# Gated mix of Hedgehog linear attention and a squared-ReLU layer: key features times values taken for two chunks of rows at a time

## The chip, the cores and the metric

The kernel runs on one core of one Trainium2 chip. The metric is device time in microseconds (us). A core has five engines that run side by side and wait for each other by semaphores: PE (TensorE, matmuls; its weight loads have a row of their own, PEld), DVE (VectorE), ACT (ScalarE), POOL (GpSimd) and SP, which here only issues DMAs. Matmuls write to PSUM, eight banks of 128 partitions x 512 floats; the other data lie in SBUF, 128 partitions wide.

## What is computed

The input x has 2048 rows of 512. Two branches are mixed with a gate per row:

```python
qkv = (x @ wqkv) -> q, k, v              # 32 heads of 16
pq, pk = q @ w_phi, k @ w_phi            # per head, 16 x 16
phi(p) = concat(softmax(p), softmax(-p)) # 32 features per head
kv = phi(pk)^T v ; z = sum over rows of phi(pk)
o = (phi(pq) kv) / (phi(pq) z + 1e-6)
a = o @ wo
b = relu(x @ w1 + b1)^2 @ w2 + b2        # 512 -> 1792 -> 512
g = sigmoid(sum(x * gate_w))
out = g * a + (1 - g) * b
```

All is in 32-bit floats. The attention has no mask, so kv and z are sums over all 2048 rows and must be complete before the first query is used.

## The kernel before

**Precision.** Large products are made in three matmuls of a faster 32-bit form: each operand is split into a high part and the low rest, and `mm3` (lines 66 to 70) adds high x high (line 68), high x low (69) and low x high (70). Lines 68 to 70 therefore stand for most of PE's time, and tiles tell apart what they belong to: `u` is the up projection x @ w1, `d` the down projection, `k`, `v`, `q` the projections of keys, values and queries, `att` the output projection. The split itself is line 60 (high part, ACT) and line 63 (low part, DVE). The feature map's weight is folded into the key and query weights beforehand (`fold`, line 142).

**Tiling and stages.** The rows are cut into 4 blocks of 512, each of 4 chunks of 128. The hidden layer's 1792 columns are cut into 14 tiles of 128, half of them per sweep. The program makes two sweeps over the rows. In each, a list of 28 steps (4 blocks x 7 hidden tiles) runs, and a step does the up projection of a hidden tile two steps ahead and the down projection of its own. Between these, the attention's work is laid by hand: `at(slot, f, ...)` puts a piece of it at a half step (lines 464 to 508), so that PE finds it in its stream between up and down projections. A scheduler then places the instructions of each engine by their dependencies and priorities; `high_priority` and `issue_after` guide it. The first sweep carries the keys and values of all 16 chunks (block b, chunk c, n = 4 b + c), the second one the queries, numerators and the output projection.

**Around the change, per chunk n of the first sweep:**

- `do_k` (lines 400 to 402): the key projection into a PSUM bank, then `exps` (191 to 210): DVE takes per head the maximum and the minimum and subtracts (lines 199 to 202) into the tile `e`, 128 x 1024; ACT takes the exponential in place (204), DVE sums it and inverts the sums (207, 209), and POOL scales `e` in place (213). The result is the chunk's key features, `phi`. The tile `e` has two buffers.
- `do_v` (404 to 407): the value projection into the same bank (there is one for this work in the first sweep, as the second bank holds the sums); ACT copies it to `vext`, in which each head has 16 values and a column of ones, set once at the start by POOL (line 126). There are two `vext` tiles, used in turn.
- `do_kv` (409 to 412) calls `kv_chunk` (217 to 224): 32 small matmuls, one per head, each with 17 columns of weights (`vext` of the head) and 32 moving columns (`phi` of the head), in four column groups of the array. All chunks add into one PSUM tile, `kvps`. They are written in plain 32-bit floats, and in the profile each of the 32 is two records of line 221. Such a run of 64 records is called a burst here.

The slots of the three are 5 + 2.9 n for `do_k`, 2 later for `do_v` and 5 later for `do_kv`, in half steps.

After the last burst `kv_done` (423 to 443) copies the sums out on DVE (line 428), sends the row of z through DRAM by SP's queue and back to all partitions (431, 434), transposes the sums on PE (439) and copies them to `kvb` (443). Then `q_phi` (226 to 243) makes the query features: the same `exps`, then POOL multiplies them by z (line 231, tile `ez`, one buffer), and so on to the row's denominator. `transposed` (247 to 257) turns them by a DVE transpose and copies, of which SP issues twelve per chunk as DMAs (line 257). `numer` (263 to 287) takes the numerators by 32 narrow matmuls of two records each per pair of chunks (line 268).

Of the kernel before, what the change touches and what calls it, by code (L numbers as in the profile page):

```python
# [8 lines left out]
F32 = mybir.dt.float32  # L9
F32R = mybir.dt.float32r  # L10
AF = mybir.ActivationFunctionType
# [5 lines left out]
P = 128  # L17
S, D, H, DH, F = 2048, 512, 32, 16, 1792
# [3 lines left out]
NC = SB // P  # L22
# [2 lines left out]
LAG = 2  # L25
NG = 8
VW = DH + 1
AHEAD = 150


@with_exitstack
def tile_gated_mix(ctx: ExitStack, tc: tile.TileContext, xT, xn, wqT, wkT, wphi, wv, wo, w1, b1, w2, b2, gw, out):
    nc = tc.nc
    pool = lambda name, bufs, **kw: ctx.enter_context(tc.tile_pool(name=name, bufs=bufs, **kw))
# [5 lines left out]
    work = pool("work", 2)  # L40
    small = pool("small", 3)
# [8 lines left out]
    def bank(name):  # L50
        p = banks[taken[0] % len(banks)]
        taken[0] += 1
        return p.tile([P, 512], F32, tag="s", name=name)
# [4 lines left out]
    def split(src, hi, lo, ehi, elo):  # L58
        if ehi is nc.scalar:
            i = nc.scalar.activation(hi, src, AF.Copy)  # L60
        else:
            i = ehi.tensor_copy(hi, src)
        elo.tensor_tensor(lo, src, hi.bitcast(F32), ALU.subtract)  # L63
        return i

    def mm3(o, a, b, sa, sb, first, last):
        (ah, al), (bh, bl) = a, b
        nc.tensor.matmul(o, ah[:, sa], bh[:, sb], start=first, stop=False)  # L68
        nc.tensor.matmul(o, ah[:, sa], bl[:, sb], start=False, stop=False)  # L69
        return nc.tensor.matmul(o, al[:, sa], bh[:, sb], start=False, stop=last)  # L70
# [36 lines left out]
        return xs  # L107

    st, up_w, down_w = {}, {}, {}
    hold = pool("hold", 2)  # L110
    ident = const.tile([P, P], F32, name="ident")
    make_identity(nc, ident)
    b1c = const.tile([P, NF], F32, name="b1c")
# [6 lines left out]
    nc.gpsimd.memset(kvb, 0.0)  # L120
    part = dram.tile([NB * NC, P, D], F32, name="part")
    zrow = dram.tile([2 * D], F32, name="zrow")
    vext = [hold.tile([P, H * VW], F32, tag="vz", name=f"vext{i}") for i in range(2)]
    heads = lambda v: v.rearrange("p (h v) -> p h v", v=VW)
    for v in vext:
        nc.gpsimd.memset(heads(v)[:, :, DH:VW], 1.0)
    zbc = []
# [10 lines left out]
    def fold(loaded, nm, k):  # L138
# [6 lines left out]
        lo = wpool.tile([P, 512], F32R, tag=f"wal{k}", name=f"w{nm}l{k}")  # L145
        with tc.high_priority(offset=AHEAD):
            split(ps, hi, lo, nc.scalar, nc.vector)
# [36 lines left out]
    def project(c, xs, ws, nm):  # L184
        ps = bank(nm)
        sc = slice(c * P, (c + 1) * P)
        for k in range(NK):
            mm3(ps, xs[k], ws[k], sc, ALL, k == 0, k == NK - 1)
        return ps

    def exps(ps):

        pv = ps.rearrange("p (h f) -> p h f", f=DH)
        mx = small.tile([P, H], F32, tag="mx", name="mx")
        mn = small.tile([P, H], F32, tag="mn", name="mn")
        e = work.tile([P, H, 2, DH], F32, tag="e", name="e", bufs=2)
        bc = lambda t: t.unsqueeze(2).to_broadcast([P, H, DH])
        with tc.high_priority(offset=AHEAD):
            nc.vector.tensor_reduce(mx, pv, AX.X, ALU.max)  # L199
            nc.vector.tensor_reduce(mn, pv, AX.X, ALU.min)  # L200
            nc.vector.tensor_tensor(e[:, :, 0, :], pv, bc(mx), ALU.subtract)
            nc.vector.tensor_tensor(e[:, :, 1, :], bc(mn), pv, ALU.subtract)  # L202
        ef = e.rearrange("p h t f -> p (h t f)")
        nc.scalar.activation(ef, ef, AF.Exp)  # L204
        e3 = e.rearrange("p h t f -> p (h t) f")
        sm = small.tile([P, 2 * H], F32, tag="sm", name="sm")
        nc.vector.tensor_reduce(sm, e3, AX.X, ALU.add)  # L207
        r = small.tile([P, 2 * H], F32, tag="r", name="r")
        nc.vector.reciprocal(r, sm)  # L209
        return e3, r  # L210

    def scaled(e3, w, eng):
        eng.tensor_tensor(e3, e3, w.unsqueeze(2).to_broadcast([P, 2 * H, DH]), ALU.mult)  # L213
        return e3.rearrange("p h f -> p (h f)")


    def kv_chunk(n, kvps, phi, v):
        for i in range(NG):
            for j in range(4):
                h = 8 * (i % 4) + 4 * (i // 4) + j  # L220
                nc.tensor.matmul(kvps[32 * j:32 * j + VW, 32 * i:32 * i + 32], v[:, h * VW:(h + 1) * VW],  # L221
                                 phi[:, 32 * h:32 * h + 32],
                                 start=(n == 0 and i == 0), stop=(n == NB * NC - 1),
                                 skip_group_check=True)

    def q_phi(n, ps):
        e3, r = exps(ps)
        ez = work.tile([P, 2 * H, DH], F32, tag="ez", name="ez", bufs=1)
        for half in range(2):
            hs = slice(half * H, (half + 1) * H)  # L230
            nc.gpsimd.tensor_tensor(ez[:, hs, :], e3[:, hs, :], zbc[half], ALU.mult)  # L231
        dz = small.tile([P, 2 * H], F32, tag="dz", name="dz")
        nc.vector.tensor_reduce(dz, ez, AX.X, ALU.add)
        nc.vector.tensor_tensor(dz, dz, r, ALU.mult)
        d2 = dz.rearrange("p (h t) -> p h t", t=2)
        den = small.tile([P, H], F32, tag="den", name="den")
        nc.vector.scalar_tensor_tensor(den, d2[:, :, 0], 1e-6, d2[:, :, 1], ALU.add, ALU.add)
        nc.vector.reciprocal(den, den)
        nc.vector.tensor_scalar(den, den, gate[:, n:n + 1], None, ALU.mult)
        w = small.tile([P, H, 2], F32, tag="w", name="w")  # L240
        nc.vector.tensor_tensor(w, r.rearrange("p (h t) -> p h t", t=2),
                                den.unsqueeze(2).to_broadcast([P, H, 2]), ALU.mult)
        return scaled(e3, w.rearrange("p h t -> p (h t)"), nc.vector)
# [19 lines left out]
    def numer(pt):  # L263
# [17 lines left out]
        for r in range(2):  # L281
            oh = work.tile([P, 512], F32R, tag=f"oh{r}", name="oh", bufs=1)
            ol = work.tile([P, 512], F32R, tag=f"ol{r}", name="ol", bufs=1)
            with tc.high_priority(offset=AHEAD):
                split(pss[r], oh, ol, nc.scalar, nc.vector)
# [112 lines left out]
            st["x", b] = load_x(b % NB)  # L398

    def do_k(b, c):  # L400
        e3, r = exps(project(c, st["x", b], st["wa"], "k"))
        st["phi", c] = scaled(e3, r, nc.gpsimd)

    def do_v(b, n, c):
        ps = project(c, st["x", b], st["wb"], "v")
        with tc.high_priority(offset=AHEAD):
            nc.scalar.activation(heads(vext[n % 2])[:, :, :DH], ps.rearrange("p (h f) -> p h f", f=DH), AF.Copy)

    def do_kv(n, c):
        if n == 0:  # L410
            st["kv"] = ps_b.tile([P, 2 * P], F32, tag="s", name="kvps")
        kv_chunk(n, st["kv"], st["phi", c], vext[n % 2])

    def do_q(b, n, c):
        phi = q_phi(n, project(c, st["x", b], st["wa"], "q"))
        if c % 2 == 0:
            st["pt", n // 2] = work.tile([P, 2, 4, NG, 32], F32, tag="phiT", name="phiT", bufs=1)
        transposed(phi, st["pt", n // 2], c % 2)
# [4 lines left out]
    def kv_done():  # L423
        kvps, kvs = st["kv"], row()[:, :2 * P]
        nc.gpsimd.memset(kvs, 0.0)
        for j in range(4):
            s = slice(32 * j, 32 * j + VW)
            nc.vector.tensor_copy(kvs[s, :], kvps[s, :])
# [3 lines left out]
        for half in range(2):  # L432
            z = hold.tile([P, H * VW], F32, tag="vz", name=f"z{half}")[:, :D]
            nc.sync.dma_start(z, zrow[half * D:(half + 1) * D].partition_broadcast(P))
# [10 lines left out]
    def finish(n, c):  # L445
# [5 lines left out]
        t = st["f", n]  # L451
        with tc.high_priority(offset=AHEAD):
            nc.vector.tensor_tensor(t, ps, t, ALU.add)
# [10 lines left out]
    def at(slot, f, *a):  # L464
        steps.setdefault(int(slot), []).append(lambda: f(*a))
# [10 lines left out]
    for b in range(NB):  # L476
        for c in range(NC):
            s = b * SL + 3 * c - 3 if b else 7 + c
            at(s, gate_load, b * NC + c)
            at(s + 3, gate_chunk, b * NC + c)  # L480
        at(b * SL + 4, do_x, b + 1)
        for c in range(NC):
            n = b * NC + c
            s = 5 + 2.9 * n
            at(s, do_k, b, c)
            at(s + 2, do_v, b, n, c)
            at(s + 5, do_kv, n, c)
    base = (NB - 1) * SL
    at(46, do_wT, wqT)
    for k in range(NK):  # L490
# [8 lines left out]
    for p in range(NB * NC // 2):  # L499
        n, s = 2 * p, 54 + 6 * p  # L500
# [30 lines left out]
    for t, (sw, b, i) in enumerate(work_list):  # L531
# [14 lines left out]
        for c in range(NC):  # L546
            n = b * NC + c
# [10 lines left out]
            for j, s in enumerate(halves if n == NB * NC - 1 and done else (ALL,)):  # L558
                with tc.high_priority(offset=AHEAD):
                    nc.vector.scalar_tensor_tensor(o[:, s], dps[c][:, s], rest[:, n:n + 1], o[:, s], ALU.mult, ALU.add)  # L560
# [49 lines left out]
```

## Time and profile before

| | us |
|---|---|
| median of 3 runs | 533.31 |
| lowest and highest of them | 532.88, 533.75 |
| the profiled execution, its own time | 533.63 |
| its span in the profile | 531.8 |

| engine | busy us | share of the span |
|---|---|---|
| DVE | 355.9 | 67% |
| ACT | 234.7 | 44% |
| POOL | 76.8 | 14% |

A row of a timeline gives the start from the span's beginning, the length, the engine, the line, the operation, output and inputs with their sizes, how many instructions it merges, and in brackets the engine's idle time before it with what released it. The length of a merged row goes from the first start to the last end, and instructions of PE overlap: their starts tell the pace, their lengths hold what is in the pipe. A row of a group gives after its shape the count, then busy us and mean ns of one, then the engine's idle time before such instructions. The sixteen bursts start at 59.86, 68.91, 83.39, 97.88, 112.37, 126.85, 141.34, 155.83, 170.31, 184.80, 202.10, 211.15, 225.63, 240.12, 256.34 and 270.88 us.

### The profile page before, as it was taken

How to read it: one execution, taken by the hardware profiler on the slowest of the kernel's cores; microseconds unless marked ns; L12 is line 12 of the kernel's file. 1: busy time of each engine (PE TensorE's matmuls, PEld its weight loads, DVE VectorE, ACT ScalarE, POOL GpSimd, SP SyncE). 2: the span in 40 equal slices, each digit the busy share in tenths (PEclk: the TensorE clock that was granted, in tenths of full speed). 3: DMA queues.
4: the chain of work that ended last, by engine and by line, in shares of the span. 5: the costliest groups of instructions: out<-in, count | busy, mean ns of one | idle time of the engine just before them, and what ended most of it. 6: DMA issues, size and time to landing. Idle time of an engine off the chain costs nothing.

```text
span 531.8 us, 8944 instructions
## 1 busy us (share of the span) xinstructions
PE 521.5 (98%) x3475; PEld 417.5 (79%) x3475; DVE 355.9 (67%) x608; ACT 234.7 (44%) x404; POOL 76.8 (14%) x60
## 2 busy tenths in 40 slices
PE   8998999999999999999999999999999999999997
PEld 3886888888888887887878878787887878787775
DVE  4688536743465434567579998998878887779423
ACT  3874333622435224254654564353435353535230
POOL 2001111111110011011103121202111111112000
PEclk9999999999999999999999999999999999999999
DMA  7974004200042000415346113134102311023102
GB/s 236 297 240 138 2 0 160 76 6 1 1 159 70 10 1 21 160 41 160 88 139 222 35 41 122 53 118 137 40 22 79 119 51 30 22 70 100 49 1 79
DMA packets 30834, 45.16 MB, mean 85 GB/s; under 512 B 5704, under 2 KB 12360, under 8 KB 30792
## 3 DMA queue, kind: packets, MB, share of 16 engines
q1 hardware_dynamic: 30328, 44.20, 27.0%
q8 instruction: 27, 0.44, 0.3%
q10 hardware_dynamic: 432, 0.39, 0.2%
q14 instruction: 15, 0.12, 0.1%
q0 software_dynamic: 32, 0.01, 0.0%
HBM read 29.89 MB, written 8.39 MB: 72 GB/s over the span
## 4 chain that ended last, share of the span: by engine, by line
PE 72%; DVE 10%; DMA 6%; SPq 5%; ACT 3%; POOL 2%; issue 2%; DVEq 0%; ACTq 0%; POOLq 0%
PE u L68 7%; PE d L69 7%; PE d L70 7%; PE d L68 7%; PE u L70 7%; PE u L69 7%; SPq L257 4%; PE v L68 3%; PE k L68 3%; PE v L69 3%; PE v L70 3%; PE k L70 3%; PE k L69 3%; PE kvps L221 2%; DMA in<-in_xT 2%; PE att L68 2%
## 5 line engine op out<-in xcount | busy, mean ns | idle before, releaser
L303 ACT ACTIVATE r<-u,b1c 128x512 f32<-128x512 f32 x56 | 38.5, 687 | 151.3 <-PE u L70 148.0
L68 PE MATMUL d<-w2h,hh 128*128 128x512 f32 x224 | 87.5, 391 | 0.0
L69 PE MATMUL d<-w2l,hh 128*128 128x512 f32 x224 | 87.3, 390 | 0.0
L70 PE MATMUL d<-w2h,hl 128*128 128x512 f32 x224 | 87.1, 389 | 0.0
L68 PE MATMUL u<-xh,w1h 128*128 128x512 f32 x220 | 86.8, 395 | 0.1
L70 PE MATMUL u<-xh,w1l 128*128 128x512 f32 x220 | 85.7, 390 | 0.5 <-DVE w1l L63 0.5
L69 PE MATMUL u<-xl,w1h 128*128 128x512 f32 x220 | 85.8, 390 | 0.0
L63 DVE TENSOR_TENSOR hl<-r,hh 128x512 fp32r<-128x512 f32 x56 | 43.0, 769 | 54.8 <-ACT hh L60 54.7
L231 POOL TENSOR_TENSOR ez<-e,z 128x512 f32<-128x512 f32 x32 | 41.4, 1317 | 188.3 <-ACT e L204 188.3
L213 POOL TENSOR_TENSOR e<-e,r 128x1024 f32<-128x1024 f32 x16 | 32.3, 2017 | 205.0 <-DVE r L209 158.3
L207 DVE TENSOR_REDUCE sm<-e 128x64 f32<-128x1024 f32 x32 | 39.0, 1218 | 28.5 <-ACT e L204 28.4
L68 PEld LDWEIGHTS u<-xh,w1h 128*128 128x128 f32 x220 | 41.3, 188 | 12.0 <-issue 1.6
L70 PEld LDWEIGHTS d<-w2h,hl 128*128 128x128 f32 x224 | 42.0, 188 | 8.7
L68 PEld LDWEIGHTS d<-w2h,hh 128*128 128x128 f32 x224 | 42.0, 188 | 8.7
L69 PEld LDWEIGHTS d<-w2l,hh 128*128 128x128 f32 x224 | 42.1, 188 | 8.6
L70 PEld LDWEIGHTS u<-xh,w1l 128*128 128x128 f32 x220 | 41.3, 188 | 9.5 <-DVE w1l L63 0.9
L69 PEld LDWEIGHTS u<-xl,w1h 128*128 128x128 f32 x220 | 41.3, 188 | 8.2
L204 ACT ACTIVATE e<-e 128x1024 f32<-128x1024 f32 x32 | 33.8, 1055 | 23.7 <-DVE e L202 23.5
L255 ACT ACTIVATE phiT<-tb 32x256 f32<-32x256 f32 x64 | 26.5, 413 | 35.1 <-DVE tb L249 34.4
L60 ACT ACTIVATE hh<-r 128x512 fp32r<-128x512 f32 x56 | 35.2, 628 | 1.3
L304 ACT ACTIVATE r<-r 128x512 f32<-128x512 f32 x56 | 35.1, 627 | 1.0
L199 DVE TENSOR_REDUCE mx<-k 128x32 f32<-128x512 f32 x16 | 11.0, 688 | 26.3 <-PE k L70 26.3
(106 smaller groups left out, 888.5 us busy)
## 6 DMA issues: line engine op xcount, KB each, us to landing
in<-in_xT SPq DMA_DIRECT2D x32, 256.0 KB, 3.9
in<-in_w SPq DMA_DIRECT2D x24, 256.0 KB, 3.2
phiT<-tb SPq DMA_DIRECT2D x192, 32.0 KB, 1.8
row<-in_xn SPq DMA_DIRECT2D x16, 256.0 KB, 3.2
part<-row SPq DMA_DIRECT2D x16, 256.0 KB, 2.0
row<-part SPq DMA_DIRECT2D x16, 256.0 KB, 3.5
out<-row SPq DMA_DIRECT2D x15, 256.0 KB, 2.2
row<-in_wkT SPq DMA_DIRECT2D x4, 256.0 KB, 6.0
```

What stands on the lines that cost most here:

```text
L60: i = nc.scalar.activation(hi, src, AF.Copy)
L63: elo.tensor_tensor(lo, src, hi.bitcast(F32), ALU.subtract)
L68: nc.tensor.matmul(o, ah[:, sa], bh[:, sb], start=first, stop=False)
L69: nc.tensor.matmul(o, ah[:, sa], bl[:, sb], start=False, stop=False)
L70: return nc.tensor.matmul(o, al[:, sa], bh[:, sb], start=False, stop=last)
L204: nc.scalar.activation(ef, ef, AF.Exp)
L207: nc.vector.tensor_reduce(sm, e3, AX.X, ALU.add)
L213: eng.tensor_tensor(e3, e3, w.unsqueeze(2).to_broadcast([P, 2 * H, DH]), ALU.mult)
L231: nc.gpsimd.tensor_tensor(ez[:, hs, :], e3[:, hs, :], zbc[half], ALU.mult)
L255: nc.scalar.activation(dst, src, AF.Copy)
L303: nc.scalar.activation(r, ps, AF.Relu, bias=b1c[:, fc:fc + 1])
L304: nc.scalar.activation(r, r, AF.Square)
```

## The change

`do_kv` is no longer called for each chunk but after each second one, at that chunk's slot, and then does two chunks one after the other. For this the features and values of three chunks are kept: `vext` has three tiles, used in turn by n modulo 3; the key features use the two buffers of `e` for n modulo 3 = 0 and 1 and the one buffer of `ez` for n modulo 3 = 2, and are remembered by n in place of c. The pool of `vext` also gives the tiles for z, so these may take other buffers. Three small tiles of `q_phi` get two buffers in place of three.

```diff
+NV = 3
...
-    hold = pool("hold", 2)
+    hold = pool("hold", NV)
...
-    vext = [hold.tile([P, H * VW], F32, tag="vz", name=f"vext{i}") for i in range(2)]
+    vext = [hold.tile([P, H * VW], F32, tag="vz", name=f"vext{i}") for i in range(NV)]
...
-    def exps(ps):
+    def exps(ps, tag="e"):
...
-        e = work.tile([P, H, 2, DH], F32, tag="e", name="e", bufs=2)
+        e = work.tile([P, H, 2, DH], F32, tag=tag, name="e", bufs=2 if tag == "e" else 1)
...
-        dz = small.tile([P, 2 * H], F32, tag="dz", name="dz")
+        dz = small.tile([P, 2 * H], F32, tag="dz", name="dz", bufs=2)
...
-        den = small.tile([P, H], F32, tag="den", name="den")
+        den = small.tile([P, H], F32, tag="den", name="den", bufs=2)
...
-        w = small.tile([P, H, 2], F32, tag="w", name="w")
+        w = small.tile([P, H, 2], F32, tag="w", name="w", bufs=2)
...
     def do_k(b, c):
-        e3, r = exps(project(c, st["x", b], st["wa"], "k"))
-        st["phi", c] = scaled(e3, r, nc.gpsimd)
+
+        n = b * NC + c
+        e3, r = exps(project(c, st["x", b], st["wa"], "k"), "ez" if n % NV == NV - 1 else "e")
+        st["phi", n] = scaled(e3, r, nc.gpsimd)
...
-            nc.scalar.activation(heads(vext[n % 2])[:, :, :DH], ps.rearrange("p (h f) -> p h f", f=DH), AF.Copy)
-
-    def do_kv(n, c):
+            nc.scalar.activation(heads(vext[n % NV])[:, :, :DH], ps.rearrange("p (h f) -> p h f", f=DH), AF.Copy)
+
+    def do_kv(n):
         if n == 0:
             st["kv"] = ps_b.tile([P, 2 * P], F32, tag="s", name="kvps")
-        kv_chunk(n, st["kv"], st["phi", c], vext[n % 2])
+        for m in (n, n + 1):
+            kv_chunk(m, st["kv"], st["phi", m], vext[m % NV])
...
-            at(s + 5, do_kv, n, c)
+            if c % 2:
+                at(s + 5, do_kv, n - 1)
```

## The prediction

> **What bounds the kernel now.** I read the page first, then the busy time by stretch, then TensorE's waits, and last the timeline around the work that moves.
>
> ```profile
> span 531.8 us, 8944 instructions
> ...
> PE 521.5 (98%) x3475; PEld 417.5 (79%) x3475; DVE 355.9 (67%) x608; ACT 234.7 (44%) x404; POOL 76.8 (14%) x60
> ...
> PE   8998999999999999999999999999999999999997
> ...
> PEclk9999999999999999999999999999999999999999
> ```
>
> TensorE (PE) is busy in every slice, at the full granted clock, and nothing else comes near it. The stretches say the same of the part of the kernel that the change touches, from 60 to 270 us (third number of a row: PE busy, then PEld, DVE, ACT, POOL):
>
> ```profile
> 60.00:270.00 210.00, 209.43 (x1841) 170.71 (x1833) 111.81 (x183) 85.41 (x138) 28.71 (x15) 1.00 0.20 63
> 270.00:320.00 50.00, 49.48 (x304) 39.55 (x303) 43.95 (x76) 26.60 (x47) 10.41 (x8) 1.00 0.34 106
> ```
>
> In those 210 us PE is idle for 0.57, DVE works 53% of the time and POOL 14%. PE's waits for other engines are few, and the largest lies at the start, before any key-times-values burst (the second is the first numerators' wait for their transposed features):
>
> ```profile
> PE k L68 <- ACT vext L407: 1.2, 1, 1.2
> ...
> PE num L268 <- DMA phiT<-tb: 1.1, 2, 0.6
> ```
>
> So what counts is how many microseconds PE's own stream takes. A busy PE is not a PE at its peak, though, so I read start-to-start steps. Around one burst (columns: start, length, engine, line):
>
> ```profile
> 126.31 0.39 PE L69 MATMUL d<-w2l,hh 128*128 128x512 f32 x1
> 126.53 0.39 PE L70 MATMUL d<-w2h,hl 128*128 128x512 f32 x1
> 126.85 0.73 PE L221 MATMUL kvps<-e,vext 128*17 128x32 f32 x64
> 127.52 0.50 PE L68 MATMUL v<-wvh,xh 128*128 128x512 f32 x1
> 127.85 0.40 PE L69 MATMUL v<-wvl,xh 128*128 128x512 f32 x1
> ```
>
> A 512-column matmul follows its neighbour after about 0.227 us (126.31 to 126.53 and so on). Into the burst the step is 0.32, from the burst's start to the next projection 0.67, and that projection's first matmul takes 0.33 instead of 0.227. From 126.53 to 127.85 are 1.32 us, where two plain steps would take 0.454: **one burst costs PE 0.866 us**. Where the same projection follows a down matmul with no burst between, nothing is lost at the boundary:
>
> ```profile
> 196.34 0.39 PE L70 MATMUL d<-w2h,hl 128*128 128x512 f32 x1
> 196.57 0.39 PE L68 MATMUL v<-wvh,xh 128*128 128x512 f32 x1
> 196.79 0.39 PE L69 MATMUL v<-wvl,xh 128*128 128x512 f32 x1
> ```
>
> Steps of 0.23 and 0.22: so this cost belongs to the burst alone. The group of all sixteen:
>
> ```profile
> L221 PE MATMUL kvps<-e,vext 128*17 128x32 f32 x1024 | 11.7, 196 | 0.0
> ...
> L221 PEld LDWEIGHTS kvps<-e,vext 128*17 128x17 f32 x1024 | 9.8, 96 | 5.6 <-issue 5.6
> ```
>
> 1024 records are 16 bursts of 64 (32 matmuls of the program, two records each), and each finds the weight path idle for 5.6/16 = 0.35 us before it, released by nothing that another engine did. That is a switch between big and small matmuls, not a wait.
>
> **The change, part by part.** *Removed:* the eight bursts of even chunks as separate stops, 8 x 0.866 = 6.93 us. *Added:* the same 64 records at the end of each odd burst. Their price is the pitch inside a burst. Over the whole burst it is (0.73 - 0.19)/63 = 8.6 ns, 0.19 being the length of the last one. I looked at the two ends of it separately, since a burst twice as long has more of its late part. The first rows below are the part that had started by 127.11, and what was still running at 127.45:
>
> ```profile
> 126.85 0.44 PE L221 MATMUL kvps<-e,vext 128*17 128x32 f32 x33
> ...
> 127.26 0.33 PE L221 MATMUL kvps<-e,vext 128*17 128x32 f32 x16
> ```
>
> Early: (0.44 - 0.19)/32 = 7.8 ns. Late: (0.33 - 0.19)/15 = 9.3 ns. It slows a little and does not stop. 64 records more cost 0.50 at the early pitch, 0.60 at the late one; I take 0.55, the mean of the whole burst. Each pair then saves 0.866 - 0.55 = 0.32 us (0.27 to 0.37), **eight pairs 2.5 us (2.1 to 2.9)**.
>
> [...]
>
> *A wait inside the burst.* The second chunk's first matmul keeps its wait for POOL's scaling of its features. It now stands in mid-burst; behind it in PE's stream are the burst's second half, then the next projection and all that follows, and DVE and ACT wait for those. The data are long there: chunk 3's features and values, used in the burst at 97.88:
>
> ```profile
> 85.06 1.94 POOL L213 TENSOR_TENSOR e<-e,r 128x1024 f32<-128x1024 f32 x1 [12.65 <-DVE r L209]
> ...
> 87.11 0.60 ACT L407 ACTIVATE vext<-v 128x512 f32<-128x512 f32 x1 [0.63 <-PE v L70]
> ...
> 97.88 0.73 PE L221 MATMUL kvps<-e,vext 128*17 128x32 f32 x64
> 98.54 0.50 PE L68 MATMUL v<-wvh,xh 128*128 128x512 f32 x1
> ```
>
> Ready 10.2 us early, and odd bursts don't move. What a satisfied wait costs in mid-burst no row shows. Lower bound 0, as at 196.57, where the projection also carries waits; upper bound the 0.12 us between the last record's start (126.85 + 0.73 - 0.19 = 127.39) and the projection at 127.52, eight times 0.96 us. I take 0, the row that is a met wait and nothing else.
>
> *What PE meets sooner.* Where an even burst is gone, the value projection behind it comes 0.87 us earlier after its own chunk's key projection, and needs the one bank from which DVE reads the keys. Before, at chunk 2's burst, and at chunk 14's, where the bank is last read for the folded query weight:
>
> ```profile
> 79.87 0.68 DVE L202 TENSOR_TENSOR e<-mn,k 128x512 f32<-128x512 f32 x1
> ...
> 84.06 0.50 PE L68 MATMUL v<-wvh,xh 128*128 128x512 f32 x1
> ...
> 254.97 0.68 DVE L63 TENSOR_TENSOR wql<-foldq,wqh 128x512 fp32r<-128x512 f32 x1
> ...
> 257.00 0.50 PE L68 MATMUL v<-wvh,xh 128*128 128x512 f32 x1
> ```
>
> The bank is free 3.5 us ahead in the first case and 1.35 in the second, so 0.87 fits in both: 0. Without that cover a pair would give back what is missing of it, at most its 0.32.
>
> *The third buffers.* Key features now go through the two "e" buffers and, for every third chunk, the "ez" one, which nothing else uses before the queries; values through three. So chunk n writes where chunk n-3 was, and n-3 is read at the latest in the burst at n-2's old place, which is the one that freed the buffer before. No wait is added or taken away. The third ones-memset on POOL (half of the 0.23 below) sits in front of POOL's weight split, behind 4.60 us of idle: 0.
>
> ```profile
> 2.55 0.23 POOL L126 MEMSET vext<- 128x32 f32 x2
> 7.38 1.00 POOL L63 TENSOR_TENSOR w1l<-row,w1h 128x384 fp32r<-128x384 f32 x1 [4.60 <-DVE w1h L62]
> ```
>
> *The handover to the queries.* The order of instructions in the changed program differs elsewhere only near the end of the first sweep: DVE's four copies of the sums come as two, then the low part of a hidden tile, then two; the two transposes of the sums stand one down group and one up matmul later. Before:
>
> ```profile
> 272.09 1.72 DVE L428 COPY row<-kvps 17x256 f32<-17x256 f32 x4
> 273.83 0.69 DVE L63 TENSOR_TENSOR hl<-r,hh 128x512 fp32r<-128x512 f32 x1
> ...
> 273.49 0.39 PE L70 MATMUL d<-w2h,hl 128*128 128x512 f32 x1
> 273.95 0.41 PE L439 MATMUL kvt<-ident,row 128*128 128x128 f32 x2
> ...
> 276.91 0.86 SPq L434 DMA_DIRECT2D z<-zrow  x2
> ...
> 282.27 2.56 POOL L231 TENSOR_TENSOR ez<-e,z 128x512 f32<-128x512 f32 x2 [23.82 <-ACT e L204]
> ```
>
> The last copy ends some 0.6 to 1.0 us later after the burst; the transposes come 4 x 0.227 = 0.9 later, so PE's stop there (0.46, of which some 0.32 is a switch) stays. The sums' row goes through DRAM on SP's queue: z is issued at 276.91, some 5 us before POOL uses it, and POOL was released by ACT. Value 0, bounds -0.15 (stop gone) and +0.5 (POOL held by a late z, and DVE behind it).
>
> *Sum.* The profiled execution took 533.63 us, 1.83 beyond its span: 533.63 - 2.5 = 531.1. It lies 0.32 above the median of the three runs, 533.31; on that base **530.8 us**, a span near 529.3.
>
> **The rivals.**
>
> *The late half of a long burst runs slower (slower than before).* If what feeds PE has only one chunk's burst in hand, records 65 to 128 come at the rate of supply. The slowest pitch of small matmuls that I find is the numerators':
>
> ```profile
> 342.64 1.09 PE L268 MATMUL num<-phiT,kvb 64*32 64x256 f32 x32
> 343.66 0.50 PE L68 MATMUL u<-xh,w1h 128*128 128x512 f32 x1
> ```
>
> (1.09 - 0.38)/31 = 23 ns. 64 x 0.023 = 1.47 us against 0.866 removed: +0.61 a pair, +4.9 in all, 538.2. It turns the sign from 0.866/64 = 13.5 ns on. For it: the pitch does rise within a burst. Against: to 9.3 only, and the numerators are eight times as wide. 8 in 100.
>
> *The gain is given back in the second sweep.* From 270 to 320 us DVE is busy for 43.95 of 50 us, and the first numerators wait for transposed features. If that chain ran by its own time, PE would only wait 2.5 us longer: 533.3. Against: the chain starts with the query projection and the last down group of the sweep, both PE's, so it moves along. 8 in 100.
>
> *The handover is late*, by its +0.5: 531.3. 6 in 100. *The wait in mid-burst costs its upper bound*: 530.8 + 0.96 = 531.8. 8 in 100. That the change does not do what it says is excluded by the program's order: eight bursts of two chunks stand there, at the places of the odd ones.
>
> **How the numbers follow.** The forecast keeps 70 in 100. Low end: 2.9 saved, 0.15 at the handover and the runs' own 0.44: 529.8. High end: 2.1 saved, less 0.96 and 0.5, 532.7, plus 0.2 for the runs: 532.9. That leaves out the slow late half and most of the give-back, 16 in 100. A measurement of this kernel can tell about 0.2%, 1.07 us, from no change. Faster by more: forecast, handover and mid-burst wait, 84, less 2 for runs at the edge: 0.82. Within: 0.10. Slower: 0.08.
>
> **What would show it.** In the changed profile: kvps in bursts of 128 records, some 1.28 us long (0.73 + 0.55), eight of them; the same steps of 0.32 and 0.33 at their ends; steps of 0.23 where even bursts were; the weight path's idle before kvps near 2.8 us, over 8 times; PE's waits for other engines as before. Wrong would be: a burst of 1.6 us or more, a pause at its 65th record, or PE waiting longer for phiT or for the bank of the projections.

## The result, and the profile after

| | before | after |
|---|---|---|
| median of 6 runs each, taken side by side, us | 533.96 (532.88 to 535.33) | 530.42 (529.82 to 530.70) |
| ratio, with its 95% interval | | 0.9937 [0.9923, 0.9951] |
| profiled execution, us | 533.63 | 529.97 |
| its span, us | 531.8 | 528.2 |

The changed kernel is faster by 0.5 to 0.8%. The first lines of its page (busy us and share of the span for each engine, then the granted clock in 40 slices), and the stretch from 60 to 270 us:

```profile
span 528.2 us, 8945 instructions
...
PE 519.0 (98%) x3475; PEld 417.6 (79%) x3475; DVE 356.5 (68%) x608; ACT 234.1 (44%) x404; POOL 77.0 (15%) x61
...
PEclk9999999999999999999999999999999999999999
```

```profile
60.00:270.00 210.00, 209.86 (x1914) 172.65 (x1913) 114.26 (x187) 88.23 (x143) 28.84 (x15) 1.00 0.21 66
```

The number of PE's matmuls is the same, 3475: no work is gone. PE is still the bound at the full granted clock, with 0.14 us idle in that stretch where it had 0.57. (The counts of matmuls in it, 1914 against 1841, say little: all sixteen chunks' records fall into it now, and fifteen chunks' did before.)

The bursts' groups, from the page's costliest groups, and PE's waits for other engines (us in total, times, longest):

```profile
L223 PE MATMUL kvps<-e,vext 128*17 128x32 f32 x1024 | 10.3, 197 | 0.0
...
L223 PEld LDWEIGHTS kvps<-e,vext 128*17 128x17 f32 x1024 | 9.4, 96 | 2.8 <-issue 2.8
```

```profile
PE k L69 <- ACT vext L411: 1.1, 1, 1.1
...
PE num L270 <- DMA phiT<-tb: 1.1, 2, 0.6
...
PE kvt L444 <- DVE row L433: 0.4, 1, 0.4
```

The weight path's idle before the bursts went from 5.6 to 2.8 us: eight times 0.35 instead of sixteen. The first numerators wait as long as before; the wait for the copies of the sums (kvt) is new in the list; the first row, for a value tile, lies at the start as it did before. The timeline around the first burst, and where an even burst had stood before:

```profile
66.67 0.39 PE L71 MATMUL d<-w2h,hl 128*128 128x512 f32 x1
66.99 1.29 PE L223 MATMUL kvps<-e,vext 128*17 128x32 f32 x128
68.22 0.50 PE L69 MATMUL v<-wvh,xh 128*128 128x512 f32 x1
68.56 0.40 PE L70 MATMUL v<-wvl,xh 128*128 128x512 f32 x1
...
81.72 0.39 PE L71 MATMUL u<-xh,w1l 128*128 128x512 f32 x1
81.95 0.39 PE L69 MATMUL v<-wvh,xh 128*128 128x512 f32 x1
82.17 0.39 PE L70 MATMUL v<-wvl,xh 128*128 128x512 f32 x1
```

From 66.67 to 68.56 are 1.89 us, two plain steps are 0.454, so a burst of two chunks costs 1.436 us. Two bursts had cost 2 x 0.866 = 1.732. **A pair saves 0.296 us, eight pairs 2.4.** The pitch is (1.29 - 0.19)/127 = 8.7 ns over all 128 records, and the 65th stands in no row of its own. Where the even burst is gone, the steps are 0.23 and 0.22.

Near the end of the first sweep, DVE and then PE:

```profile
268.16 0.69 DVE L64 TENSOR_TENSOR w1l<-in,w1h 128x512 fp32r<-128x512 f32 x1 [2.65 <-ACT w1h L61]
268.76 0.84 DVE L433 COPY row<-kvps 17x256 f32<-17x256 f32 x2
269.61 0.69 DVE L64 TENSOR_TENSOR hl<-r,hh 128x512 fp32r<-128x512 f32 x1
270.32 0.86 DVE L433 COPY row<-kvps 17x256 f32<-17x256 f32 x2
```

```profile
267.69 0.50 PE L69 MATMUL d<-w2h,hh 128*128 128x512 f32 x1
...
270.55 0.39 PE L69 MATMUL u<-xh,w1h 128*128 128x512 f32 x1
271.33 0.41 PE L444 MATMUL kvt<-ident,row 128*128 128x128 f32 x2 [0.40 <-DVE row L433]
```

The copies start 268.76 - 267.69 = 1.07 us after the first matmul behind the last burst (before 272.09 - 271.54 = 0.55): DVE, in its order, holds a weight's low part ahead of them and waits 2.65 us for ACT. The step into the transposes is 0.78 us where it was 0.46.

One stop went away that has nothing to do with the bursts, the first product of the folded query weight. Before, then after:

```profile
252.75 1.13 PE L142 MATMUL foldq<-row 128*128 128x128 f32 x8 [0.57 <-PE d L68]
```

```profile
249.17 1.05 PE L143 MATMUL foldq<-row 128*128 128x128 f32 x8
```

To see where the 3.6 us of the two spans are, I cut each trace at two PE matmuls: the second key projection's first, and the first large one behind the last burst.

| us | start | between | rest of the span |
|---|---|---|---|
| before | 46.94 | 224.60 | 260.3 |
| after | 45.91 | 221.77 | 260.5 |
| after, profiled again | 46.90 | 221.93 | 260.5 |

2.8 us came from the middle: 2.4 from the pairs, and the remaining 0.4 is put down to the query weight's stop. The rest got 0.2 longer, at the handover. 1.0 came from the start, where the weights are loaded; in the second profile of the same kernel this part was gone. So the traces bear out about 2.5 us, the runs about 3.5 (2.6 to 4.1 by the interval).

### The profile page after: what moved, and what is told of

It reads as the page before. It is cut to its first block, busy times and chain, and to the rows that moved or that the text cites. A ratio compares the mean times of both kernels' runs of the same rounds, so it can differ in the third digit from the quotient of the medians.

```text
span 528.2 us, 8945 instructions
## 1 busy us (share of the span) xinstructions
PE 519.0 (98%) x3475; PEld 417.6 (79%) x3475; DVE 356.5 (68%) x608; ACT 234.1 (44%) x404; POOL 77.0 (15%) x61
## 4 chain that ended last, share of the span: by engine, by line
PE 63%; DVE 15%; DMA 7%; ACT 5%; SPq 5%; issue 2%; POOL 2%; DVEq 0%; POOLq 0%; ACTq 0%
PE u L69 6%; PE u L71 6%; PE u L70 6%; PE d L71 6%; PE d L70 6%; PE d L69 6%; SPq L259 4%; PE k L69 3%; PE v L69 2%; PE k L70 2%; PE k L71 2%; PE v L70 2%; PE v L71 2%; DMA in<-in_w 2%; PE att L69 2%
## 5 line engine op out<-in xcount | busy, mean ns | idle before, releaser
L208 DVE TENSOR_REDUCE sm<-e 128x64 f32<-128x1024 f32 x32 | 39.0, 1217 | 28.5 <-ACT e L205 28.3
L566 DVE SCALAR_TENSOR_TENSOR row<-d,rest,row 128x512 f32<-128x512 f32 (+1 forms) x33 | 22.4, 731 | 8.5 <-PE d L71 8.5
```

## The experiments

My theory: the gain is eight fewer switches of PE between large and small matmuls, 0.30 us each. Rivals: the added buffers, or the place of things, not the merging; and, for longer bursts, that something which feeds PE runs out. All kernels compute the whole result. Of each edit the main lines are shown. Each was compared with runs of the kernel before on the same chip.

**The buffers alone.** The changed kernel with a burst for each chunk again:

```diff
-        for m in (n, n + 1):
-            kv_chunk(m, st["kv"], st["phi", m], vext[m % NV])
+        kv_chunk(n, st["kv"], st["phi", n], vext[n % NV])
...
-            if c % 2:
-                at(s + 5, do_kv, n - 1)
+            at(s + 5, do_kv, n)
```

> The third buffers of values and key features, with one burst per chunk as before. The order of PE's instructions is that of the kernel before. Theory (the gain comes from eight switches fewer between large and small matmuls): no gain, ratio 1.000 +- 0.002 to the kernel before; sixteen bursts of 64 records, 0.73 us each, 5.6 us of weight-path idle before them. Rival (the buffers loosen DVE, ACT and POOL, or the start of the kernel is shorter for them): ratio near 0.9935 as the whole change, with PE's first key projection after the first value projection near 45.9 us instead of 46.9.

Measured: 533.17, ratio 0.9981 [0.9967, 0.9994]. The middle took 224.86 us, like before's 224.60, and its weight path idles as before's did:

```profile
L223 PEld LDWEIGHTS kvps<-e,vext 128*17 128x17 f32 x1024 | 9.8, 96 | 5.6 <-issue 5.6
```

The gain comes with the merging. What the runs show of 0.3 to 1.8 us for the buffers alone is in no part of its trace (span 531.9 against 531.8; the query weight's stop is 0.74 us in it, 0.17 longer), and stays open.

**More switches instead of fewer.** The kernel before, each burst cut in two halves of 32 records a slot apart:

```diff
-        for i in range(NG):
+        for i in groups:
...
-            at(s + 5, do_kv, n, c)
+            at(s + 4, do_kv, n, c, range(0, 4))
+            at(s + 5, do_kv, n, c, range(4, 8))
```

> The kernel before with each chunk's burst cut in two halves of 32 records, the first half one half step earlier: the same matmuls, sixteen entries and exits more. Theory: each entry and exit costs 0.30 us besides the pitch (2 x 0.866 of the kernel before less 1.436 that a burst of two chunks costs after the change), so 16 x 0.30 = +4.8 us, ratio 1.009, weight-path idle before bursts 11.2 us over 32 times. Rival (a burst costs by its records, 0.866/64 = 13.5 ns each): no change, ratio 1.000.

Measured: 536.70, ratio 1.0046 [1.0032, 1.0060]. A half burst in the timeline, and the group:

```profile
60.80 0.39 PE L70 MATMUL d<-w2h,hl 128*128 128x512 f32 x1
61.12 0.43 PE L221 MATMUL kvps<-e,vext 128*17 128x32 f32 x32
61.47 0.50 PE L68 MATMUL k<-wkh,xh 128*128 128x512 f32 x1
61.81 0.39 PE L69 MATMUL k<-wkl,xh 128*128 128x512 f32 x1
```

```profile
L221 PEld LDWEIGHTS kvps<-e,vext 128*17 128x17 f32 x1024 | 9.8, 97 | 11.3 <-issue 11.3
```

A half costs 1.01 - 0.454 = 0.556 us, two 1.11, so a cut costs 1.11 - 0.866 = 0.246; sixteen cuts 3.9, and the middle grew by 3.6 (to 228.21). The idle doubled, 32 times 0.35. The sign and the idle are as expected, the size is smaller. A cut costs less than a merge saves because two halves hold only early records, which come at 7.8 ns: the fixed part of a half, 0.556 - 32 x 0.0078 = 0.31, is that of a whole burst, 0.866 - 64 x 0.0086 = 0.32.

**The changed kernel once more**, with no edit, beside these:

> The changed kernel once more, for comparison on the same chip. Theory: ratio to the kernel before 0.993 to 0.995, the bursts and the handover as in its first profile; the 1.0 us by which its first profile was ahead already before the first burst is the loads' luck in that execution and differs this time. Rival: that 1.0 us is of the change and is there again.

Measured: 531.08, ratio 0.9945 [0.9926, 0.9964], span 529.3. The middle repeats (221.93); the start does not.

**Four chunks in a burst.** If fewer switches are all, this gains more. Buffers of the second sweep hold the added chunks:

```diff
-NV = 3
+NV = 5
...
-        for m in (n, n + 1):
+        for m in range(n, n + NC):
...
-            if c % 2:
-                at(s + 5, do_kv, n - 1)
+            if c == NC - 1:
+                at(s + 5, do_kv, n - c)
```

> One burst for four chunks, 256 records, at the fourth chunk's slot; five buffers each, the further ones in tiles that the second sweep uses. Theory: four switches fewer than the changed kernel, 4 x 0.30 = -1.2 us against it, ratio to the kernel before near 0.991, each burst 0.73 + 3 x 0.55 = 2.4 us at a pitch of 8.6 ns. Rival (a long burst outruns what feeds PE, which 128 records did not show yet): records late in the burst at 13.5 ns or more, no gain against the changed kernel or a loss.

Measured: 544.72, ratio 1.0200 [1.0173, 1.0227]. The expectation fell, and its sign with it. PE's waits, the timeline around the first burst ("more" is a borrowed buffer), and the stretch behind it by windows (length, then PE busy, PEld, DVE, ACT, POOL; last granted clock, DMA share, GB/s):

```profile
PE kvps L225 <- issue: 9.3, 4, 2.5
```

```profile
96.59 0.30 PE L225 MATMUL kvps<-e,more 128*17 128x32 f32 x13
99.14 0.60 PE L225 MATMUL kvps<-e,more 128*17 128x32 f32 x49 [2.25 <-issue]
99.67 0.69 PE L69 MATMUL v<-wvh,xh 128*128 128x512 f32 x1
100.16 0.63 PE L70 MATMUL v<-wvl,xh 128*128 128x512 f32 x1
```

```profile
99.70:103.50 3.80, 3.80 (x14) 2.97 (x11) 1.60 (x6) 0.00 (x0) 0.00 (x0) 0.55 0.58 169
```

Each of the four bursts has one pause of 2.23 to 2.50 us, put down to "issue": no engine and no transfer released it. Behind it PE runs at a granted clock of 0.55, with steps of 0.43 instead of 0.227 us. Pause and slow clock together cost some 3.6 to 3.9 us a burst in this execution: the middle took 236.23, where 221.77 less four more switches of 0.296 would be 220.6, and 1.25 us of the difference are a stop at the query weight, which the changed kernel does not have.

A pause after 207, 221, 247 and 240 records is no fixed length. But counted through the whole program, PE's records (weight loads, matmuls and the few semaphore instructions that the trace has for PE) stand at 1217, 2241, 3265 and 4289: each 193 beyond a multiple of 256. The page of the changed kernel has a queue for it (packets, MB, share):

```profile
q8 instruction: 27, 0.44, 0.4%
```

27 packets of 16 KB: PE's instructions come in blocks, and 3475 matmuls with as many loads are 27 blocks of 256. A burst of 256 records is 512 instructions and so holds a whole block, which PE runs through in 1.1 us (128 records at 8.7 ns). *New theory: where a burst runs through a whole block, the next one is not there in time, and PE stops at its edge.* Rivals: a fixed length that PE can hold, or the borrowed buffers.

**Four chunks, the program shifted by a quarter block.** Five of the eleven warm-up matmuls at the start are replaced by 37 tiny ones, 64 instructions more:

```diff
-        idle(11)
+        idle(5)
+        for _ in range(37):
+            nc.tensor.matmul(st["warm"][:32, :32], z[:, :32], z[:, :32], start=True, stop=True)
+        idle(1)
```

> Bursts of four chunks, with 37 tiny matmuls in place of five warm-up matmuls at the start, so that everything behind stands 64 PE instructions later in the blocks of 256. Theory of blocks: four pauses again, since 512 instructions always hold a whole block, but each 64 instructions (32 records) earlier in its burst: after 175, 189, 215 and 208 records of kvps in place of 207, 221, 247 and 240. Rival (the wait of a later chunk, or the data): the pauses stay at 207, 221, 247 and 240.

Measured in a single run: 544.61 against 534.02 before. First burst:

```profile
96.26 1.70 PE L225 MATMUL kvps<-e,vext 128*17 128x32 f32 x175
99.99 0.41 PE L225 MATMUL kvps<-e,vext 128*17 128x32 f32 x17 [2.03 <-issue]
```

The pauses stand after 175, 189, 215 and 208 records, each 32 earlier: they belong to the program's count, not to the burst's length or its buffers.

**Three chunks in a burst**, 192 records, with four sets of buffers, bursts at chunks 2, 5, 8, 11, 14 and 15:

```diff
-NV = 3
+NV = 4
...
-            if c % 2:
-                at(s + 5, do_kv, n - 1)
+            if n % 3 == 2 or n == NB * NC - 1:
+                at(s + 5, do_kv, n - n % 3, n)
```

> Bursts of three chunks (five of 192 records, then the last chunk alone), four buffers each. Theory from the burst of four chunks (PE runs its instructions from blocks of 256, asks for the next block when it enters one, and gets it 3.5 us later or more; a block that a burst runs through whole lasts 1.1 us): 192 records are 384 instructions, and in bursts 2 to 5 a whole block lies inside the burst: pauses of 1.3 to 2.5 us in four of the five bursts, at records where the count of PE's instructions is 193 modulo 256, and matmuls of 0.427 us behind them: ratio 1.00 to 1.025. Rival (a pause comes only from a burst longer than some length above 192 records, or from the wait of the fourth chunk): no pause, two switches fewer than the changed kernel, ratio 0.9925.

Measured: 543.93, ratio 1.0191 [1.0159, 1.0223]. The first two bursts:

```profile
83.93 1.85 PE L225 MATMUL kvps<-e,vext 128*17 128x32 f32 x192
...
127.33 0.90 PE L225 MATMUL kvps<-e,vext 128*17 128x32 f32 x84
130.25 0.76 PE L225 MATMUL kvps<-e,vext 128*17 128x32 f32 x42 [2.03 <-issue]
```

Four pauses again, 9.3 us together, in the second to fifth burst, again at counts 193 beyond a multiple of 256. The first burst has none, though a whole block lies in it too: it comes to that block 23 instructions after its start, the second burst 44 after. An estimate from these two bursts: PE can run a block some 4 us after it stood 50 instructions short of the block ahead. For 23, that point falls 27 instructions before the burst, 13.5 large matmuls or 3.1 us, and with 1.2 us in the burst the block is there. For 44 it falls 3 large matmuls or 0.7 us before, and 0.7 + 0.2 + 1.1 + the 2.03 of the pause are again 4.0. The 50 is fitted to these pauses, not measured; with it the time comes out as 3.4 to 4.2 us in the pauses of the four-chunk kernels. That PE asks for a block when it enters the one ahead, as the expectation has it, no run shows.

The traces also hold the packets themselves, and they stand where the theory needs them. At each of the twelve pauses of the three kernels with long bursts, a packet for PE begins between 0.42 us before the pause and 0.59 us after its start, and PE goes on 1.26 to 1.61 us after that packet has ended. At the first burst of three chunks, which has no pause, the packet ended at 82.91, a microsecond before the burst began. And in the kernel before, the four packets between 65 and 112 us, with only large matmuls in the microseconds ahead of them, begin 36 to 41 records short of an edge, and the 50 of the estimate lie ahead of them.

**Three chunks, shifted by half a block**, with the edit above and 69 tiny matmuls instead of 37 (128 instructions more). Then no burst holds a whole block:

> The kernel with bursts of three chunks, with 69 tiny matmuls in place of five of the eleven warm-up matmuls at the start, while PE waits for its first loads: everything behind stands 128 PE instructions later in the instruction blocks, nothing else changes from the first burst on. Theory of blocks: no block lies whole inside a burst any more, no pauses; from the second key projection to the end of the last burst 0.6 us less than the changed kernel's 221.8 to 221.9; ratio 0.992 to 0.994, with up to 1 us more at the start if the tiny matmuls hold up the first real one. Rival (length or the buffers cause the pauses): the same pauses as without the shift.

Measured: 533.43, ratio 0.9980 [0.9962, 0.9998]. The bursts pass at once; the end of the second one, the weight path and one of PE's waits (the weight path's 1.4 us are four of the six bursts at 0.35; the other two begin with values in the borrowed buffer and have a row of their own, with 0.7):

```profile
124.00 1.27 PE L225 MATMUL kvps<-e,vext 128*17 128x32 f32 x126
```

```profile
L225 PEld LDWEIGHTS kvps<-e,vext 128*17 128x17 f32 x768 | 7.0, 96 | 1.4 <-issue 1.4
```

```profile
PE foldq L145 <- PE d L69: 0.8, 1, 0.8
```

The same bursts, the same buffers, only another place in the blocks, and 10.5 us are back. The middle is 221.74, no better than with pairs: the two switches saved, 0.6 us, went into the query weight's stop of 0.8, which the changed kernel had lost. But the part behind the last burst had grown by some 4 us, which the expectation did not have. Was it the three chunks or the shift?

**The changed kernel, shifted by half a block**, with the same 69 tiny matmuls:

> The changed kernel (two chunks) with the 69 tiny matmuls of the shifted kernel of three chunks: 128 PE instructions later in the blocks. Theory of blocks: a burst of 128 records is 256 instructions, and PE has taken some 50 instructions ahead, so wherever a burst falls a block's end comes 3.5 us or more after its start: no pause, 221.8 to 221.9 us from the second key projection to the end of the last burst, as without the shift. Open beside it: the shifted kernel of three chunks took 4.3 us longer from the last burst to the end, with one issue step of 1.54 us on SP among the 24 of 0.63 and a stop of 2.55 us at the first numerators; if that is of the shift (where PE's blocks are loaded), it is there again and the tail is near 260 us, otherwise 256.2 us.

Measured: 534.03, ratio 0.9993 [0.9978, 1.0009]: at the median the whole gain is gone. (The 50 instructions in the expectation are the fitted estimate above; that PE has taken them ahead was not measured.) The ten executions spread: six took 533.86 to 535.50, with a mean granted clock of 0.996 or 0.997, and four took 531.95 to 532.30, with 0.998 to 1.000, which keeps some 1.9 us of the gain. The profiled one is of the six. The bursts are innocent: no pause, the middle 221.73. The loss lies in the second sweep, as in the run before, so it belongs to the shift. PE's waits, the first numerators, the stretch behind them, and SP's queue of transposes before and at the place (the length of a row holds all its issues):

```profile
PE num L270 <- DMA phiT<-tb: 3.2, 2, 2.0
```

```profile
310.03 0.62 PE L270 MATMUL num<-phiT,kvb 64*32 64x256 f32 x2
312.62 1.40 PE L270 MATMUL num<-phiT,kvb 64*32 64x256 f32 x30 [1.97 <-DMA phiT<-tb]
```

```profile
314.50:316.50 2.00, 2.00 (x6) 1.58 (x5) 1.83 (x4) 1.97 (x6) 0.00 (x0) 0.50 0.12 33
```

```profile
300.24 3.12 SPq L259 DMA_DIRECT2D phiT<-tb  x5
...
302.77 3.45 SPq L259 DMA_DIRECT2D phiT<-tb  x4
```

SP issues one transpose every 3.12/5 = 0.62 us; at 302.77 four took 3.45, of which one step is 1.59. That step began when a packet of PE's instruction queue began, at 303.40. The transposes' chain lost 1.0 us there, the first numerators stopped for 1.97, and the clock went to 0.50 behind that. In the traces of before and after, the instruction packets near this place lie at 293.13 and 316.0, and at 288.91 and 312.45, outside their stretches of issues (297.6 to 312.8, and 294 to 309). The thirteen traces together have 58 issues on SP of more than 0.9 us, where most take 0.3 to 0.6. 57 of them ended 0.27 to 0.39 us after a packet for PE had ended, and the last one 0.19 us after a packet of another instruction queue. Such issues stand in the second sweep of before and after too, at places where the numerators do not wait; here one fell on the first numerators' chain. So long issues and packets belong together; that the packet holds up the issue, and not a third thing both, is inferred, and it was not tried by itself.

**Two buffers instead of three.** The merged bursts need them, or do they?

```diff
-NV = 3
+NV = 2
...
-        e3, r = exps(project(c, st["x", b], st["wa"], "k"), "ez" if n % NV == NV - 1 else "e")
+        e3, r = exps(project(c, st["x", b], st["wa"], "k"), "e")
```

> The changed kernel with two buffers of values and key features in place of three: one burst for two chunks, but the next chunk's features can be written only after the burst. Theory: the gain of the long burst stays, 2.4 us, and is lost to new waits: the next value projection stands three or four up matmuls (0.7 to 0.9 us) behind the burst and needs DVE's two subtractions (2 x 0.6 us) that now start only when the burst has ended, so 0.3 to 0.6 us a burst, 2.4 to 4.8 us in all: ratio to the kernel before 1.000 to 1.005. PE's waits show v <- DVE e some eight times. Rival (the third buffer is needed only to keep order, its waits are hidden): ratio 0.994 as with three.

Measured: 534.24, ratio 0.9999 [0.9984, 1.0014], middle 225.20. PE's waits, and PE behind a burst:

```profile
PE v L69 <- DVE e L203: 2.5, 3, 1.2
```

```profile
96.89 1.29 PE L223 MATMUL kvps<-e,vext 128*17 128x32 f32 x128
98.11 0.50 PE L69 MATMUL u<-xh,w1h 128*128 128x512 f32 x1
...
100.55 0.47 PE L69 MATMUL v<-wvh,xh 128*128 128x512 f32 x1 [1.25 <-DVE e L203]
```

The bursts are as short as ever, but the next chunk's features can only be written behind them, so DVE reads the keys' bank late and the value projection waits for it. Behind seven of the eight bursts the step into that projection is 0.48 to 1.64 us in place of 0.227, some 3.2 us together, which is nearly all of the 3.4 by which the middle grew. The third buffers are what keeps the gain.

**The handover.** Two tries to get back its 0.2 us: first the four copies with high priority; then the same, with the weights of one hidden tile of the second sweep loaded two half steps later.

```diff
+        with tc.high_priority(offset=AHEAD):
             for j in range(4):
...
-        at(base + 2 * i + 2, do_ffn, NFH + i)
+        at(base + 2 * i + (4 if i == 4 else 2), do_ffn, NFH + i)
```

> The changed kernel with the four copies of the sums put ahead of the hidden tile's low part on DVE, so that they stand together again. Theory: PE's stop before the transposes of the sums, 0.78 us after the change against 0.46 before, shrinks by 0.3 to 0.4, the tail from the last burst to the end goes back from 256.25 to 256.0 us: -0.2 to -0.3 us against the changed kernel, ratio to the kernel before near 0.9935, not to be told from the changed kernel's by the runs. Rival (the later copies cost nothing): same tail of 256.25 us.

> The kernel with the copies of the sums together, and one hidden tile's weights of the second sweep loaded two half steps later, by which ACT makes the next weight's high part ahead of the relu again, as before the change. Theory: the copies of the sums started 1.07 us after the last burst's end in the changed kernel against 0.55 before, since DVE stood idle for 2.65 us behind the low part of a weight that ACT made late; with ACT's order restored they start at about 0.55, the first numerators come 41.5 us after the last burst again in place of 41.85, the tail is 256.0 us: 0.3 us less than the changed kernel. Rival: the tail is set by DVE's or SP's later work and stays at 256.25 us. Too small for the runs: ratio 0.993 to 0.995 either way.

Measured: 531.18, ratio 0.9936 [0.9912, 0.9960], and 530.68, ratio 0.9942 [0.9923, 0.9961]; the part behind the last burst stayed as after's in the first and grew by 0.7 us in the second. Both missed. DVE in the second:

```profile
268.94 0.69 DVE L64 TENSOR_TENSOR w1l<-in,w1h 128x512 fp32r<-128x512 f32 x1 [1.66 <-ACT w1h L61]
269.55 1.71 DVE L434 COPY row<-kvps 17x256 f32<-17x256 f32 x4
```

The four copies now stand together, but still behind the weight's low part, which waits for ACT; they start 269.55 - 268.24 = 1.31 us after the last burst. What the handover costs was not cured, and no kernel tried was clearly faster than the changed one.

## Why the prediction was right

*A burst costs a fixed switch, not a wait: right.* Idle of 0.35 us a burst with 8, 16 and 32 bursts; the cost moves with the number of bursts in both directions.

*The added half at 0.55 us: right, a little low.* It cost 1.436 - 0.866 = 0.57, so a pair saved 0.296 where 0.32 was predicted, and eight 2.4 where 2.5 was. These narrow matmuls start 8.7 ns apart over 128 records, against 8.6 over 64.

*The late half does not run slower: right for 128 records, in part by luck.* I looked at the pitch, and the pitch stays. That what feeds PE has one chunk's burst in hand and no more, the rival's condition, is not shown by any run. The worry behind it was sound all the same: with 192 and 256 records PE stops, not at a slower pitch but in one pause of 2.0 to 2.9 us. A row of a 64-record burst could not show that, nor that 128 records stay below the limit (some 140 by the estimate at the end).

*The met wait in mid-burst at 0: right.* 128 records have one pitch throughout. *Even bursts gone at 0, and the third buffers at 0: right for PE's gaps*, steps of 0.23 and 0.22, and no wait for the keys' bank added; with two buffers such waits took the gain back.

*The handover at 0 (-0.15 to +0.5): the size was off, within its bounds.* It cost 0.2. I had the last copy 0.6 to 1.0 late and the transposes 0.9. The split of the copies was foreseen, but not that they would start 0.5 us later behind a weight's low part: the last copy ended 1.2 us later after the burst than before ((270.32 + 0.86 - 267.69) less (272.09 + 1.72 - 271.54)), and the transposes waited 0.40 for it.

*The gain given back in the second sweep: it did not happen here.* Numerators wait 1.1 us as before. In the shifted kernel the whole gain was lost just there, by another mechanism than I had named.

*Not foreseen:* the end of the query weight's stop (0.57 us before, none after, 0.33 when profiled again), and 1.0 us of the start. By the prediction's 2.5 us the medians would differ by 2.5; they differ by 3.5 in these runs and by 2.7 in the later ones. The traces' lasting part, 2.4 + 0.2 to 0.6 - 0.2, is 2.4 to 2.8, and what the runs have beyond that is open; part of it may be the buffers' 0.3 to 1.8. That the forecast of 530.8 lies only 0.4 from the measured 530.42 is therefore in part luck: the base of 533.31 was 0.65 below the later median of 533.96, and the difference of the medians was 1.0 above the forecast one.

## What to carry to other kernels

Where the matmul engine is the bound, count its changes between large and small matmuls: each cost 0.25 to 0.30 us here, nothing waits in it, and merging two bursts saved it as long as the buffers let the producers run on. Before making such a burst longer, count instructions: a whole block of 256 inside one burst cost some 3.6 to 3.9 us. A kernel's time may also depend on where its instruction blocks fall, so measure a change of less than one per cent at a second alignment before believing it.

## What the runs showed of the chip

*Instruction blocks.* 27 packets of 16 KB stand in the traces of before and after, beside 3475 matmuls and as many loads of PE; with the remainder of 193 modulo 256 at every pause, that gives 256 instructions to each. Pauses of 2.0 to 2.9 us stood at a block's edge in 12 of 13 bursts that held a whole block, and in none of the 16 pair bursts of the changed kernel and its shifted form, nor of the three-chunk bursts shifted by half a block. In the pair bursts an instruction started every 4.3 ns (8.7 ns for a load and a matmul). By the estimate fitted to the three-chunk bursts, 50 instructions and 4 us, a block entered up to 25 instructions into a burst is followed in time (12.5 large matmuls or 2.8 us ahead, 0.1 and 1.1 in the burst). So a burst up to some 280 instructions (140 records) is safe at any place: an estimate; no burst between 128 and 192 records was run.

*The clock.* A pause of 2.25 us was followed by a granted clock of 0.55 over 3.8 us (the four-chunk kernel), one of 1.97 by 0.50 over 2 us (the shifted kernel). Behind the second and third pause of the four-chunk kernel (2.29 and 2.23 us) it was 0.57 over 4.0 us and 0.54 over 3.7; each of these three stretches is some 1.7 us of lost work on top of the pause (0.45 x 3.8, 0.43 x 4.0, 0.46 x 3.7). It fell so behind nine of the twelve pauses of the long bursts and stayed full behind the other three (2.12, 2.34 and 2.86 us), so the pause's length alone does not decide it. What does was not shown.

*A transfer's issue beside an instruction packet.* SP's step of 0.62 us became 1.59 where a packet for PE began, and in the profiled execution the part behind the last burst took 3.8 us longer (264.3 against 260.5): a microsecond late at the head of a chain, a stop, and a slow clock behind it.
